# Splitting expert weights once and reloading the split pairs from HBM scratch

## The chip, the cores and the metric

The kernel runs on one core of one Trainium2 chip. The metric is device time in microseconds, the median of several runs. Engines are named as the profile names them: PE is TensorE (PEld its weight loads), DVE is VectorE, ACT is ScalarE, POOL is GpSimd, SP is SyncE, which here issues nearly all DMAs. A name with a q at its end (SPq) is the engine's sequencer: it waits and issues.

## The reference, cut to what matters

Attention with a compressive memory gives x; a mixture of four experts then runs on x.

```
B, H, S, D = 4, 8, 576, 64
a = softmax(causal(q @ k.T / sqrt(D)))
x = g * mem_out + (1 - g) * (a @ v)        # as (2304, 512)
N, D, E, F = 2304, 512, 4, 1024
p = domain_probs / (domain_probs.sum(-1) + 1e-9)
for e in range(E):
    h = np.maximum(x @ w1[e], 0.0)
    out += p[:, e:e+1] * (h @ w2[e])       # every token, every expert
```

All data are float32. The products keep that precision by splitting an operand into a high part (rounded to the fp32r format of TensorE) and a low part (the rest); a product is then three matmuls: high by high, high by low, low by high.

## The kernel before, in words

The tokens are cut into 9 groups of 256 (two tiles of 128 rows). Each group goes through 8 phases, one for each expert and half of F (`NPH` = 8). Group g starts at phase `START[g]` (0, 5, 8, 13, 16, 21, 24, 29, 32), so there are 40 phases (`PHASES`). In phases 0 to 4 and 37 to 39 one group is active (products of 256 columns), in phases 5 to 36 two groups are (512 columns).

One phase uses four pieces of w1 and four of w2, each 128x512 floats (256 KB). `mm1` makes h for each of the four pieces `fc` of w1: 4 x 3 matmuls each, then ACT (L769) and DVE (L770) split relu(h) into `hh` and `hl`. `mm2` makes y for each token tile: 4 x 3 matmuls with the w2 pieces, then DVE adds p*y to `acc` (L806); after a group's last phase `acc` is stored (L813).

A weight piece gets to its operand in this way. `w_dma` loads it on SP's queue into one of four staging tiles `stg` (L189 for w1, in runs of 512 bytes; L194 for w2, in runs of 2 KB). `w_prep` makes the high part (ACT L210, or POOL L212) and the low part (POOL L214; DVE for some pieces of the last four phases), then calls `w_dma` for the piece that comes four later, whose staging tile has just been read. `w_prep(i, "2")` is called after each piece of `mm1` of phase i, `w_prep(i + 1, "1")` after the tiles of `mm2` of phase i. The operands (`w1h`, `w1l`, `w2h`, `w2l`, four of each) exist once. `wseq` lists the pieces of all 40 phases in order, 320 in all: each expert's weights are loaded and split again every eight phases.

Batch 0's first 256 rows are computed in `first_run`, which also prepares the first eight pieces (on POOL). All other attention work is a list of steps of 28 tasks, interleaved with the phases by a planner with costs written by hand; a group's steps are all emitted before its first phase. A task's q, k and v come in by `t_load` (L269 and L275, tile `natall`, six or more DMAs on SP's queue), are transposed on PE (`tq`, `tk`, line L315), split, and partly copied by DMA from SBUF to SBUF (`kha`, `khb`, L342; `qz`, L361). The engines run in program order, and each DMA issue of SP waits in SP's own order until its source is ready and its destination free. The attention steps run through phase 28; later phases hold expert work alone.

Of the kernel before, what the change touches and what calls it, by code (L numbers as in the profile page):

```python
# [8 lines left out]
F32 = mybir.dt.float32  # L9
F32R = mybir.dt.float32r  # L10
# [12 lines left out]
PR = {  # L23
    "phi1": [-5, 1],
    "phi2": [-5, 7],
    "phi3": [-4, 7],
    "trq": [-3, 6.5],
    "trk": [-4, -0.5],
    "v": -2,
    "trqp": [2, 2.5],  # L30
    "qk": 0,
# [22 lines left out]
def tile_attention_moe(  # L54
# [13 lines left out]
    nc = tc.nc  # L68
    P = 128
    B, H, S, D = q.shape  # L70
    NT, DM = out.shape
    E, _, F = w1.shape
    NPAIR = H // 2
    NKD = DM // P
    HF = 4
# [20 lines left out]
    NPH = E * NHALF  # L96
    START = [g // 2 * NPH + (PR["x"] if g % 2 else 0) for g in range(NG)]
    PHASES = START[-1] + NPH
# [10 lines left out]
    def ctile(shape, dt, name):  # L109
        return cst.tile(shape, dt, tag=name, name=name)  # L110

    def f(ap):
        return ap.bitcast(F32)
# [4 lines left out]
    def wid(c):  # L118
        return min((c + 1) * P, S)
# [12 lines left out]
    for i in range(2):  # L132
        o, d = i * 13 * P, {}
# [25 lines left out]
    xl = ctile([P, NKD, 2 * GW], F32R, "xl")  # L159
    hh = [ctile([P, 2 * GW], F32R, f"hh{i}") for i in range(HF)]  # L160
    hl = [ctile([P, 2 * GW], F32R, f"hl{i}") for i in range(HF)]
    w1s = [
        (ctile([P, NKD, P], F32R, f"w1h{i}"), ctile([P, NKD, P], F32R, f"w1l{i}"))
        for i in range(HF)
    ]
    w2s = [
        (ctile([P, DM], F32R, f"w2h{i}"), ctile([P, DM], F32R, f"w2l{i}"))
        for i in range(HF)
    ]


    halves = [(i // NHALF % E, i % NHALF) for i in range(PHASES)]
    wseq = [(i, kind, fc) for i in range(PHASES) for kind in "12" for fc in range(HF)]
    NSTG = 4
    wpos = {"dma": 0, "prep": 0}
    stg = {}
# [1 line left out]
    def w_dma():  # L178
        j = wpos["dma"]
        if j >= len(wseq):  # L180
            return
        wpos["dma"] += 1
        i, kind, fc = wseq[j]
        e, hf = halves[i]
        f0 = (hf * HF + fc) * P
        t = sp.tile([P, DM], F32, tag="stg", name=f"stg{j}", bufs=NSTG)
        stg[j] = t
        if kind == "1":
            nc.sync.dma_start(  # L189
                out=t.rearrange("p (c f) -> p c f", c=NKD),  # L190
                in_=w1[e, :, f0 : f0 + P].rearrange("(c p) f -> p c f", p=P),
            )
        else:
            nc.sync.dma_start(out=t, in_=w2[e, f0 : f0 + P, :])  # L194

    def w_prep(i, kind, pool=False):
        last_ = i >= PHASES - 4
        act = (kind == "1" or i < START[1] or last_) and not pool
        j = wpos["prep"]
        if j >= len(wseq) or wseq[j][0] != i or wseq[j][1] != kind:  # L200
            return
        wpos["prep"] += 1
        fc = wseq[j][2]
        t = stg.pop(j)
        hi, lo = (w1s if kind == "1" else w2s)[fc]
        if kind == "1":
            hi = hi.rearrange("p c f -> p (c f)")
            lo = lo.rearrange("p c f -> p (c f)")
        if act:
            nc.scalar.activation(hi, t, AF.Copy)  # L210
        else:
            nc.gpsimd.tensor_scalar(hi, t, 1.0, 1.0, ALU.mult, ALU.mult)  # L212
        dve = (last_ and fc % 2) or (i < START[1] and fc < PR["lod"])
        (nc.vector if dve else nc.gpsimd).tensor_tensor(lo, t, f(hi), ALU.subtract)  # L214
        w_dma()


# [29 lines left out]
    for b, cs in RUNS[1:]:  # L247
        for a in range(NPAIR):
            t = Task()
# [146 lines left out]
    for t in tasks:  # L396
# [7 lines left out]
        for hds, c in order:  # L404
            s = Slot()
# [257 lines left out]
    def mm(n):  # L663
        return max(107.0, n / 2.4 + 2.5)
# [23 lines left out]
    for i, s in slots.items():  # L688
        w = wid(s.c)
        t = s.t  # L690
# [61 lines left out]
    def mm1(i, fc, cols, after):  # L752
        wh, wl = w1s[fc]
        pt = []

        def part(c):
            if c == 0:
                pt.append(ps.tile([P, 512], F32, tag="moe", name=f"h{i}_{fc}", bufs=3))
            for z, (w_, x_) in enumerate(((wh, xh), (wh, xl), (wl, xh))):
                nc.tensor.matmul(  # L760
                    pt[0][:, cols],
                    lhsT=w_[:, c],
                    rhs=x_[:, c, cols],
                    start=(c == 0 and z == 0),
                    stop=(c == NKD - 1 and z == 2),
                )
            if c == NKD - 1:
                h_, l_ = hh[fc][:, cols], hl[fc][:, cols]
                nc.scalar.activation(h_, pt[0][:, cols], AF.Relu)  # L769
                nc.vector.scalar_tensor_tensor(  # L770
                    l_, pt[0][:, cols], 0.0, f(h_), ALU.max, ALU.subtract
                )
                after()

        return [lambda c=c: part(c) for c in range(NKD)]

    def mm2(i, g, tt, after):
        e = halves[i][0]
        pieces = GROUPS[g][tt]
        pe = pn[:, pcol(pieces), e : e + 1]  # L780
        t0 = (g % 2) * GW + tt * P
        tk = slice(t0, t0 + P)
        pt = []

        def part(fc):
            if fc == 0:
                pt.append(ps.tile([P, 512], F32, tag="moe", name=f"y{i}_{g}_{tt}", bufs=3))
            wh, wl = w2s[fc]
            for z, (h_, w_) in enumerate(((hh, wh), (hh, wl), (hl, wh))):
                nc.tensor.matmul(  # L790
                    pt[0],
                    lhsT=h_[fc][:, tk],
                    rhs=w_,
                    start=(fc == 0 and z == 0),
                    stop=(fc == HF - 1 and z == 2),
                )
            if fc == HF - 1:
                fin()
                after()

        def fin():
            if i == START[g]:
                acc[g, tt] = sp.tile([P, DM], F32, tag="acc", name=f"acc{g}_{tt}", bufs=4)
                nc.vector.tensor_scalar(acc[g, tt], pt[0], pe, None, ALU.mult)
            else:
                nc.vector.scalar_tensor_tensor(  # L806
                    acc[g, tt], pt[0], pe, acc[g, tt], ALU.mult, ALU.add
                )
            if i == START[g] + NPH - 1:
                o0 = 0  # L810
                for b, c in pieces:
                    r0, m = b * S + c * P, rows(c)
                    nc.sync.dma_start(out=out[r0 : r0 + m, :], in_=acc[g, tt][o0 : o0 + m])  # L813
                    o0 += m

        return [lambda c=c: part(c) for c in range(HF)]

    def phase_parts(i):
        gs = [g for g in range(NG) if START[g] <= i < START[g] + NPH]
        c0 = min(g % 2 for g in gs) * GW  # L820
        cols = slice(c0, c0 + len(gs) * GW)
        out_ = []
        for fc in range(HF):
            for p_ in mm1(i, fc, cols, lambda: w_prep(i, "2")):
                out_.append((3 * mm(len(gs) * GW), p_))
        if i + 1 in START:
            out_.append((0.0, START.index(i + 1)))
        nt = 2 * len(gs)

        def after():  # L830
            for _ in range(HF // nt):
                w_prep(i + 1, "1")

        for g in gs:
            for tt in range(2):
                for p_ in mm2(i, g, tt, after):
                    out_.append((3 * mm(DM), p_))
        return out_


    def first_run():
# [226 lines left out]
        out=mask[:, 4 * P :],  # L1068
        in_=mask[:, 4 * P :],
# [24 lines left out]
    with tc.manual_schedule():  # L1094
# [8 lines left out]
        for i in range(2):  # L1103
            zeros(i)
            nc.gpsimd.memset(f(QK[i]["qz"]), 0.0)
            nc.gpsimd.memset(f(QK[i]["qa"][:, 3 * P :]), 0.0)
        phases = [phase_parts(i) for i in range(PHASES)]
        pcost = [sum(c for c, _ in ph) for ph in phases]

# [65 lines left out]
```

## Time and profile before

| what | value |
|---|---|
| median of 3 runs | 1035.13 us (1034.83 to 1036.03) |
| span of the profiled execution | 1034.4 us |
| PE busy | 1007.5 us, 97% |
| DVE, ACT, POOL busy | 688.3, 482.8, 582.6 us |
| DMA moved | 123.16 MB, mean 119 GB/s |
| mean share of time in which the 16 DMA engines worked, queue q1 (SP and ACT) | 43.3% |
| HBM read, written | 106.86 MB, 4.72 MB |

The profile gives the span from the first instruction to the last of one execution; the execution's own total is not recorded beside it, and the median of the runs is 0.7 us above the span. A busy PE is an engine with a matmul in its pipeline, so one matmul's duration (about 390 ns for 512 columns) is longer than the distance to the next.

### The profile page before, as it was taken

To read this page: it belongs to the slowest core of one execution; us is meant where nothing else is said; L and a number is where in the kernel's file an instruction comes from. 1 tells how busy PE (TensorE), PEld (TensorE's weight loads), DVE (VectorE), ACT (ScalarE), POOL (GpSimd) and SP (SyncE) were. 2 spreads that over 40 slices of the span, in tenths; PEclk is the share of its full clock that TensorE was granted. 3 is DMA by queue.
4 is the path that set the end of the run, shared out by engine and by line. 5 is a ranking of instruction groups with operands and counts; after the bars stand their busy time and mean duration, and the time that the engine had idled before them with its cause. 6 is when DMAs were issued, how large, how long until landed. Compare 5 with 4: busy or idle time off the path is not lost.

```text
span 1034.4 us, 16262 instructions
## 1 busy us (share of the span) xinstructions
PE 1007.5 (97%) x5183; PEld 846.1 (82%) x5183; DVE 688.3 (67%) x1638; ACT 482.8 (47%) x1144; POOL 582.6 (56%) x599
## 2 busy tenths in 40 slices
PE   6798999999999999999999999999999999999998
PEld 4588888888888888888888888888888888888887
DVE  6689887888777777887777867766666323222344
ACT  4476755565554555545555555444434222211234
POOL 4658566666544755467444565565553654656233
PEclk8899899999999999999999999999999999999999
DMA  6546554465434444355334544263331432333244
GB/s 139 128 129 188 154 156 114 122 165 131 114 96 120 132 130 109 88 145 140 101 94 103 139 128 119 79 174 87 92 103 57 128 102 82 123 101 94 79 142 134
DMA packets 213637, 123.16 MB, mean 119 GB/s; under 512 B 100656, under 2 KB 187696, under 8 KB 213552
## 3 DMA queue, kind: packets, MB, share of 16 engines
q1 hardware_dynamic: 213264, 121.85, 43.3%
q8 instruction: 42, 0.69, 0.3%
q10 hardware_dynamic: 288, 0.27, 0.1%
q14 instruction: 43, 0.35, 0.1%
HBM read 106.86 MB, written 4.72 MB: 108 GB/s over the span
## 4 chain that ended last, share of the span: by engine, by line
PE 87%; DVE 6%; POOL 3%; issue 2%; ACT 1%; DMA 1%; SPq 0%; POOLq 0%; ACTq 0%; DVEq 0%
PE y L790 36%; PE h L760 35%; PE sp L553 4%; PE pt L315 4%; PE o L654 4%; POOL w1l L214 1%; PE tk L315 1%; PE o L501 1%; PE tq L315 1%; DVE sf L943 1%; PE tp L315 1%; POOL w2l L214 1%; PE sp L427 1%; DVE qp L310 1%; DVE rn L308 0%
## 5 line engine op out<-in xcount | busy, mean ns | idle before, releaser
L214 POOL TENSOR_TENSOR w1l<-stg,w1h 128x512 fp32r<-128x512 f32 x152 | 198.2, 1315 | 314.3 <-ACT w1h L210 258.5
L760 PE MATMUL h<-xh,w1h 128*128 128x512 f32 (+1 forms) x640 | 248.5, 388 | 0.0
L760 PE MATMUL h<-xh,w1l 128*128 128x512 f32 (+1 forms) x640 | 237.8, 372 | 0.0
L790 PE MATMUL y<-w2h,hh 128*128 128x512 f32 x576 | 237.2, 412 | 0.0
L760 PE MATMUL h<-xl,w1h 128*128 128x512 f32 (+1 forms) x640 | 236.8, 370 | 0.0
L790 PE MATMUL y<-w2h,hl 128*128 128x512 f32 x576 | 226.8, 394 | 0.0
L790 PE MATMUL y<-w2l,hh 128*128 128x512 f32 x576 | 226.0, 392 | 0.7 <-POOL w2l L214 0.7
L214 POOL TENSOR_TENSOR w2l<-stg,w2h 128x512 fp32r<-128x512 f32 x152 | 198.8, 1311 | 46.4 <-ACT w2h L210 35.7
L769 ACT ACTIVATE hh<-h 128x512 fp32r<-128x512 f32 (+1 forms) x160 | 88.7, 555 | 237.9 <-PE h L760 236.5
L770 DVE SCALAR_TENSOR_TENSOR hl<-h,hh 128x512 fp32r<-128x512 f32 (+1 forms) x160 | 101.8, 636 | 125.4 <-ACT hh L769 124.2
L806 DVE SCALAR_TENSOR_TENSOR acc<-y,pn,acc 128x512 f32<-128x512 f32 x126 | 94.2, 748 | 73.5 <-PE y L790 72.7
L760 PEld LDWEIGHTS h<-xh,w1l 128*128 128x128 f32 x640 | 121.3, 190 | 21.4
L760 PEld LDWEIGHTS h<-xh,w1h 128*128 128x128 f32 x640 | 121.6, 190 | 16.5 <-issue 0.2
L760 PEld LDWEIGHTS h<-xl,w1h 128*128 128x128 f32 x640 | 121.9, 191 | 15.8
L790 PEld LDWEIGHTS y<-w2h,hl 128*128 128x128 f32 x576 | 108.7, 189 | 25.1 <-DVE hl L770 1.0
L790 PEld LDWEIGHTS y<-w2l,hh 128*128 128x128 f32 x576 | 109.5, 190 | 18.6 <-POOL w2l L214 1.1
L790 PEld LDWEIGHTS y<-w2h,hh 128*128 128x128 f32 x576 | 109.3, 190 | 18.0
L596 ACT ACTIVATE pth<-pt 128x384 fp32r<-128x384 f32 (+3 forms) x128 | 50.4, 420 | 103.4 <-PE pt L315 102.9
L210 ACT ACTIVATE w1h<-stg 128x512 fp32r<-128x512 f32 x156 | 93.6, 624 | 9.2 <-DMA stg<-in_moe_w_dram 8.4
L212 POOL TENSOR_SCALAR w2h<-stg 128x512 fp32r<-128x512 f32 x128 | 81.8, 639 | 15.9 <-PE y L790 15.9
L561 DVE CUSTOM_DVE_ANT_0 s<-sp,mask 128x384 f32<-128x384 f32 (+1 forms) x96 | 52.9, 563 | 13.4 <-PE sp L553 12.7
L315 PE MATMUL pt<-ident,s 128*128 128x128 f32 (+1 forms) x376 | 60.9, 273 | 0.4 <-DVE s L464 0.4
(152 smaller groups left out, 1425.1 us busy)
## 6 DMA issues: line engine op xcount, KB each, us to landing
stg<-in_moe_w_dram SPq DMA_DIRECT2D x320, 256.0 KB, 2.9
natall<-in_k_dram SPq DMA_DIRECT2D x34, 128.0 KB, 2.7
out_dram<-acc SPq DMA_DIRECT2D x16, 256.0 KB, 2.2
natall<-in_v_dram SPq DMA_DIRECT2D x32, 128.0 KB, 2.6
natall<-in_q_dram SPq DMA_DIRECT2D x60, 64.0 KB, 2.7
kha<-kha SPq DMA_DIRECT2D x16, 128.0 KB, 3.2
khb<-khb SPq DMA_DIRECT2D x16, 128.0 KB, 3.0
natall<-in_k_dram SPq DMA_DIRECT2D x28, 64.0 KB, 2.4
```

Of the source, the lines that this page charges most:

```text
L210: nc.scalar.activation(hi, t, AF.Copy)
L212: nc.gpsimd.tensor_scalar(hi, t, 1.0, 1.0, ALU.mult, ALU.mult)
L214: (nc.vector if dve else nc.gpsimd).tensor_tensor(lo, t, f(hi), ALU.subtract)
L315: nc.tensor.transpose(dst, src, ident[0:n, 0:n])
L553: nc.tensor.matmul(pt[:, 0 : b_ - a], lhsT=q_, rhs=qk[k_][:, a:b_], start=y == 0, stop=y == len(pairs) - 1,)
L561: nc.vector.tensor_tensor_reduce(s.s[:, a:b_], pt[:, 0 : b_ - a], mask[:, m0 : m0 + b_ - a] if c < 4 else mask4[:, a:b_], 1.0, 3.0e38, ALU ...
L596: nc.scalar.activation(dh, src, AF.Copy)
L760: nc.tensor.matmul(pt[0][:, cols], lhsT=w_[:, c], rhs=x_[:, c, cols], start=(c == 0 and z == 0), stop=(c == NKD - 1 and z == 2),)
L769: nc.scalar.activation(h_, pt[0][:, cols], AF.Relu)
L770: nc.vector.scalar_tensor_tensor(l_, pt[0][:, cols], 0.0, f(h_), ALU.max, ALU.subtract)
L790: nc.tensor.matmul(pt[0], lhsT=h_[fc][:, tk], rhs=w_, start=(fc == 0 and z == 0), stop=(fc == HF - 1 and z == 2),)
L806: nc.vector.scalar_tensor_tensor(acc[g, tt], pt[0], pe, acc[g, tt], ALU.mult, ALU.add)
```

## The change

Only the 64 pieces of phases 0 to 7 are loaded and split (`wseq` ends at `NPH`). High and low part of a piece now lie side by side in one tile `wpair` of 128x2x512 floats. After each split the pair is noted in `wpend`; the next call of `w_prep` first stores what is noted to a DRAM tile of its own (`w_store`, 512 KB on SP's queue). From phase 8 on `w_load` brings a pair from its DRAM tile straight into the operands, again on SP's queue, 512 KB each: a w1 pair of phase i+1 right after `mm1` of phase i has used that piece, the four w2 pairs together after the last tile of `mm2` of phase i. The rule for the last four phases (`last_`: ACT and DVE help) is gone.

```diff
+    wpair = {k_: [ctile([P, 2, DM], F32R, f"w{k_}{i}") for i in range(HF)] for k_ in "12"}
...
-    wseq = [(i, kind, fc) for i in range(PHASES) for kind in "12" for fc in range(HF)]
+    wseq = [(i, kind, fc) for i in range(NPH) for kind in "12" for fc in range(HF)]
+    wkeep = {}
+    wpend = []
...
+    def w_store():
+        while wpend:
+            key, t = wpend.pop(0)
+            d = tc.dram_tile([P, 2, DM], F32, name="wk%d%s%d" % key)
+            wkeep[key] = d
+            nc.sync.dma_start(out=d, in_=f(t))
+
+    def w_load(i, kind, fc):
+        if NPH <= i < PHASES:
+            nc.sync.dma_start(out=f(wpair[kind][fc]), in_=wkeep[i % NPH, kind, fc])
+
     def w_prep(i, kind, pool=False):
-        last_ = i >= PHASES - 4
-        act = (kind == "1" or i < START[1] or last_) and not pool
+        w_store()
+        act = (kind == "1" or i < START[1]) and not pool
...
-        dve = (last_ and fc % 2) or (i < START[1] and fc < PR["lod"])
+        dve = i < START[1] and fc < PR["lod"]
...
+        wpend.append((wseq[j], wpair[kind][fc]))
         w_dma()
...
-            for p_ in mm1(i, fc, cols, lambda: w_prep(i, "2")):
+            def after1(fc=fc):
+                w_prep(i, "2")
+                w_load(i + 1, "1", fc)
+
+            for p_ in mm1(i, fc, cols, after1):
...
+        left = [nt]
+
         def after():
             for _ in range(HF // nt):
                 w_prep(i + 1, "1")
+            left[0] -= 1
+            if left[0] == 0:
+                for fc in range(HF):
+                    w_load(i + 1, "2", fc)
```

`PR["lod"]` is 0, so `dve` is false in the changed kernel.

## Rows read from the trace of the kernel before

**Rows 1.** The page, engines: busy us, share of the span, instructions.
```profile
PE 1007.5 (97%) x5183; PEld 846.1 (82%) x5183; DVE 688.3 (67%) x1638; ACT 482.8 (47%) x1144; POOL 582.6 (56%) x599
```
**Rows 2.** Windows: length, then busy us of each engine, granted clock, DMA.
```profile
core 0: us, PE busy (x) PEld busy (x) DVE busy (x) ACT busy (x) POOL busy (x), PEclk, DMA share, GB/s
...
60.40:130.20 69.80, 63.37 (x411) 57.05 (x410) 62.70 (x154) 51.16 (x135) 51.77 (x52) 0.95 0.62 170
130.20:215.20 85.00, 84.67 (x449) 70.88 (x448) 71.94 (x192) 48.49 (x131) 53.53 (x63) 1.00 0.49 135
215.20:803.60 588.40, 587.36 (x3018) 493.92 (x3017) 440.55 (x1056) 294.06 (x680) 330.34 (x328) 1.00 0.43 114
803.60:996.90 193.30, 193.30 (x854) 159.94 (x854) 56.50 (x82) 44.47 (x80) 101.12 (x95) 1.00 0.36 105
996.90:1030.50 33.60, 33.60 (x216) 30.41 (x214) 16.93 (x29) 15.90 (x32) 13.03 (x10) 1.00 0.47 142
```
**Rows 3.** The chain of work that ended last, 803 us on: start, us, what.
```profile
811.88 10.88 PE y L790 x48
...
996.87 5.75 PE h L760 x48
```
**Rows 4.** Timeline of PE: the first matmul of phases 1, 5 and 8.
```profile
60.40 0.28 PE L760 MATMUL h<-xh,w1h 128*128 128x256 f32 x1
...
130.21 0.47 PE L760 MATMUL h<-xh,w1h 128*128 128x512 f32 x1
...
215.23 0.40 PE L760 MATMUL h<-xh,w1h 128*128 128x512 f32 x1
```
**Rows 5.** Waits of PE: us in total, times, longest.
```profile
PE y L790 <- POOL w2l L214: 0.7, 1, 0.7
```
**Rows 6.** The page, costliest groups: the split's instructions on ACT and POOL.
```profile
L214 POOL TENSOR_TENSOR w1l<-stg,w1h 128x512 fp32r<-128x512 f32 x152 | 198.2, 1315 | 314.3 <-ACT w1h L210 258.5
...
L210 ACT ACTIVATE w1h<-stg 128x512 fp32r<-128x512 f32 x156 | 93.6, 624 | 9.2 <-DMA stg<-in_moe_w_dram 8.4
L212 POOL TENSOR_SCALAR w2h<-stg 128x512 fp32r<-128x512 f32 x128 | 81.8, 639 | 15.9 <-PE y L790 15.9
```
**Rows 7.** The page, DMA issues: count, KB each, median us to landing.
```profile
stg<-in_moe_w_dram SPq DMA_DIRECT2D x320, 256.0 KB, 2.9
```
**Rows 8.** DMA between 60.4 and 130.2 us (phases 1 to 4).
```profile
DMA packets 20598, 11.87 MB, mean 170 GB/s; under 512 B 9169, under 2 KB 18385, under 8 KB 20591
...
stg<-in_moe_w_dram SPq DMA_DIRECT2D x33, 256.0 KB, 3.0
```
**Rows 9.** DMA between 130 and 215 us (phases 5 to 7).
```profile
DMA packets 19765, 11.47 MB, mean 135 GB/s; under 512 B 10055, under 2 KB 17479, under 8 KB 19757
...
stg<-in_moe_w_dram SPq DMA_DIRECT2D x25, 256.0 KB, 2.9
```
**Rows 10.** Windows: one lone 256 KB store of `acc`; the fastest microsecond.
```profile
1029.40:1030.30 0.90, 0.90 (x5) 0.58 (x4) 0.00 (x0) 0.00 (x0) 0.00 (x0) 1.00 0.76 291
...
1022.00:1023.00 1.00, 1.00 (x11) 1.00 (x10) 0.37 (x1) 0.51 (x2) 1.00 (x1) 1.00 1.05 395
```
**Rows 11.** DMA issues between 30 and 36 us.
```profile
stg<-in_moe_w_dram SPq DMA_DIRECT2D x4, 256.0 KB, 5.9
```
**Rows 12.** Timeline of SP: a task's k loads being issued.
```profile
73.80 0.97 SPq L269 DMA_DIRECT2D natall<-in_k_dram  x2
```
**Rows 13.** Timeline of PE: the transposes that read those k loads.
```profile
77.81 0.41 PE L315 MATMUL tk<-ident,natall 128*128 128x128 f32 x2
```
**Rows 14.** Windows: the four microseconds behind a wait of PE.
```profile
104.00:108.00 4.00, 4.00 (x20) 3.54 (x20) 2.73 (x9) 2.70 (x6) 1.76 (x2) 0.79 0.64 166
```
**Rows 15.** Timeline of DVE: one small instruction of two tasks.
```profile
47.22 0.16 DVE L308 SCALAR_TENSOR_TENSOR rn<-rn,gate 128x4 f32<-128x4 f32 x1
...
66.82 0.95 DVE L308 SCALAR_TENSOR_TENSOR rn<-rn,gate 128x4 f32<-128x4 f32 x1
```
**Rows 16.** Waits of SP's queue: us in total, times, longest.
```profile
SPq L194 <- POOL w1l L214: 251.8, 109, 12.1
```

More of the change, by code (lines that the diff above doesn't have):

```diff
@@ L161, in tile_attention_moe @@
     hl = [ctile([P, 2 * GW], F32R, f"hl{i}") for i in range(HF)]
+    wpair = {k_: [ctile([P, 2, DM], F32R, f"w{k_}{i}") for i in range(HF)] for k_ in "12"}
     w1s = [
-        (ctile([P, NKD, P], F32R, f"w1h{i}"), ctile([P, NKD, P], F32R, f"w1l{i}"))
-        for i in range(HF)
-    ]
[L166 to L169, printed above, removed]
+        tuple(t[:, z].rearrange("p (c f) -> p c f", c=NKD) for z in range(2)) for t in wpair["1"]
+    ]
+    w2s = [tuple(t[:, z] for z in range(2)) for t in wpair["2"]]
     halves = [(i // NHALF % E, i % NHALF) for i in range(PHASES)]
-    wseq = [(i, kind, fc) for i in range(PHASES) for kind in "12" for fc in range(HF)]
+    wseq = [(i, kind, fc) for i in range(NPH) for kind in "12" for fc in range(HF)]
+    wkeep = {}
+    wpend = []
     NSTG = 4
```

## The prediction

> **What bounds the kernel now.** I read the page's engine rows first: PE is busy 97% of the span, no other engine above 67% [rows 1]. The windows say where PE is not full. In phases 1 to 4 it idles 69.80 - 63.37 = 6.4 us; in phases 5 to 7 0.3 us; from phase 8 to the end of the attention work 588.40 - 587.36 = 1.0 us; after 803 us nothing [rows 2, 4]. The chain of waits agrees: late it is PE alone, 48 matmuls in 10.88 us, 0.227 us each, and 5.75 us for the 48 narrow ones of a half phase [rows 3]. While PE runs at that pace, POOL is still splitting weights (101.12 us of 193.30 [rows 2]). So the splits cost PE nothing there. In the list of waits, PE waits for a split once, 0.7 us [rows 5]. Two other things matter for this change: the DMA engines work 0.62 of the time in phases 1 to 4, 0.49 in phases 5 to 7 and 0.36 to 0.47 later [rows 2], and SP's queue is mostly held back by POOL's splits [rows 16].
>
> **What is removed.** The 256 pieces of phases 8 to 39 lose an ACT or POOL copy (0.62 to 0.64 us) and a subtraction of 1.3 us [rows 6]. That is over 300 us of POOL work, none of it on PE's path. The most that can come back is PE's idle time from phase 8 on, 1.0 us [rows 2]. I take -1.0. Lower bound of the cost: -3, if the wait of 0.7 us [rows 5] and its like also cost refills of the pipeline that count as busy; upper bound: 0.
>
> **What is added in phases 0 to 7: 64 stores of 512 KB.** SP issues them in front of the next staging load. No row shows a 4 KB row or a 512 KB transfer, so I bound the price. A lone 256 KB store moves at 291 GB/s in 0.9 us, which makes 1.80 us for 512 KB; the fastest microsecond of the trace moved 395 GB/s, which makes 524,288 / 395e3 = 1.33 us [rows 10]. I take 1.33, because these stores run in a filled queue, like that microsecond and unlike the lone one.
>
> Phases 1 to 4 (69.8 us) issue 33 staging loads and so 33 stores, beside the 11.87 MB that they move already [rows 8]. Stores: 33 x 1.33 = 43.9 us. The old transfers need at least 11.87e3 / 395 = 30.1 us and at most 0.62 x 69.8 = 43.3 us. The share counts overlapping packets twice (it is 1.05 in the fastest microsecond [rows 10]), so I take the lone store's pace, 11.87e3 / 291 = 40.8 us. Sum: 84.7 us of DMA work in 69.8 us, 14.9 too many. The bounds: 30.1 + 43.9 = 74.0, 4 too many; 43.3 + 33 x 1.80 = 102.7, 33 too many.
>
> Phases 5 to 7 have room: 11.47e3 / 291 + 25 x 1.33 = 72.7 of 85 us [rows 9, 2]. How much backlog can be carried there? The staging ring holds four pieces; four loads of 0.9 and four stores of 1.33 would be 8.9 us in the queue. I take half, 5 us. That leaves +10 us in phases 1 to 4.
>
> Why does PE feel it, though stores are needed by nobody for a long time? All transfers sit in SP's one queue. Four staging loads that are issued at the end of a burst of transfers near 30 us land after 5.9 us instead of 2.9 [rows 11, 7]; a load behind two or three stores will fare the same. What is late next is named in the rows: a task's k loads finish being issued at 74.77 us, and PE's transposes of them start at 77.81, 3.0 us later, hardly more than a landing [rows 12, 13, 7]. These transposes stand in PE's program order, so expert matmuls behind them wait too. The staging loads come late as well; then ACT's copy waits, and behind it, in ACT's order, the evictions of h and the exponentials. SP itself pays 0.97 / 2 = 0.49 us for an issue [rows 12], 16 us for 33 stores. It already waits in the same places for POOL's subtraction [rows 16], so the store brings no new wait for data.
>
> After a wait PE's clock drops: behind one of the present waits the granted clock is 0.79 of 2.4 GHz over 4 us, a loss of 0.21 x 4 = 0.8 us [rows 14]. New waits in four phases would cost 3 us. Against that, the 6.4 us that PE already idles there [rows 2] can fall together with the new waits. I count the two as equal: 0, bounds -4 and +4. Before phase 1 eight stores fall into the start, where the weights are ready long before they are used; 0, upper bound 2.
>
> The Trainium skill, "DMA: Bandwidth & Descriptors", section "Where 436 GB/s comes from", says that transfers between HBM and SBUF are held by HBM at about 358 GB/s for a core. By that figure a store would be 1.46 us, an estimate, and the sum 40.8 + 33 x 1.46 = 89.0 us, so +14 after the carried 5 in place of +10. The fastest microsecond here, 395 GB/s [rows 10], is above it.
>
> **What is added from phase 8 on: 256 loads of 512 KB** instead of 256 KB. Per full phase that is 8 x 1.33 = 10.6 us (bound 8 x 1.80 = 14.4) for 8 x 0.9 = 7.2 us before, in 21.8 us of pure expert work [rows 3, 10]. The shares of 0.43 and 0.36 [rows 2] rise by 0.15 to 0.33: not full. A w1 pair has most of a phase to arrive. The four w2 pairs are issued together when y ends: 4 x 1.33 to 4 x 1.80 plus the fixed 2.9 - 0.9 = 2.0 us gives 7.3 to 9.2 us for the last. In full phases 10.88 us of h cover that. In the three half phases the cover is 5.75 us, plus nine matmuls of y before the fourth pair is used, 2.0 us: 7.8 us [rows 3]. So 0 to 1.4 us each; I take 0, upper bound 4. SP now waits for PE at each load instead of for POOL; behind it stand the loads of later tasks and the copies `kha`, `qz`, whose sources come from PE work emitted later, so I take 0. Upper bound 5, if some q, k or v loads fall behind a burst of w2.
>
> **Sum.** -1 + 10 + 0 + 0 = +9 us on the span of 1034.4. The median of the runs is 0.7 us above the span, so 1035.1 + 9 = **1044 us**.
>
> **Rivals.**
> *The stores hide (no change).* For it: nobody needs them soon, and by the lowest bound only 4 us are too many, which the staging ring can carry into phases 5 to 7. Against it: the k loads with no slack [rows 12, 13]. Time: 1035.1 - 1 + 0 to 2 = 1034 to 1036.
>
> *Faster: DVE and POOL stop colliding.* One small DVE instruction takes 0.16 us in one task and 0.95 in another [rows 15]. If a POOL instruction holds it up, then without the splits every DVE step of the attention chain from phase 8 on is shorter. This decides only if PE waits for that chain; PE's idle 1.0 us says it does not [rows 2]. With the -3 above and hidden stores: 1032. The Trainium skill, "SBUF — State Buffer", section "Who interferes with whom", says that a DVE instruction with two SBUF inputs contends with a GpSimd instruction that reads SBUF. The 0.16 and 0.95 us agree with such a lock, but a freed DVE is not what PE lacks here.
>
> *Much slower: the loads hurt too.* Stores at 1.80 us (+33 - 5 = +28), or bursts of w2 that hold up task loads and the half phases (+9 above the sum). Time 1053 to 1063. For it: the small packets in phases 1 to 4 (9,169 of 20,598 under 512 bytes [rows 8]). Against it: later shares stay under 0.8.
>
> *The change doesn't do what it says:* the DRAM pairs are stored long before phase 8 and the loads name them directly; I see no way and give it nothing.
>
> **How the numbers follow.** Forecast (the early phases are held by DMA, +2 to +17, 1037 to 1052): 0.60. Stores hidden: 0.14. Faster: 0.10. Much slower: 0.16. A change under 0.2% (2.1 us) can't be told from none here. Slower by more: 0.60 + 0.16 = 0.76; the same 0.14; faster 0.10. For 8 in 10 I leave out the faster case and the upper half of the much slower one: 1034 to 1058; the forecast's own range is 1037 to 1052.
>
> **What would show it.** In the changed profile: DMA share near 0.9 or above from about 60 to 200 us; staging loads there landing after 4 to 7 us instead of 3.0; phase 8 starting near 225 us instead of 215.2; PE waiting at `tk` or ACT at L287 and L210 for landings. From phase 8 on, POOL under 150 us busy, stretches of PE as long as before (588 and 193 us), DMA share 0.55 to 0.7. Wrong would be: phase 8 starting at 215 us (the stores hide), or the half phases longer than 33.6 us, or PE waiting for `w2` loads after phase 8.

## The result, and the profile after

The change makes the kernel slower: 1048.88 us (median of 4 runs) against 1035.58 us (median of 4 runs of the kernel before), a ratio of 1.0128 [1.0114 to 1.0143], or +13.3 us. The forecast was 1044.0 us, with a range of 1034 to 1058 and 0.76 on slower. The profiled execution of the changed kernel took 1048.86 us for a span of 1047.1 us. Against the span before, 1034.4 us, that is +12.7 us. The distance of 0.7 us between span and median in the prediction was not that of one execution, where it is 1.8 us here.

These are rows of the changed kernel's page: the engines, the DMA share in 40 slices of 26.2 us, a group of the split, and the two new transfers (count, KB each, median us to landing).

```profile
PE 1010.6 (97%) x5183; PEld 848.9 (81%) x5183; DVE 640.4 (61%) x1622; ACT 406.5 (39%) x1000; POOL 201.1 (19%) x247
...
DMA  6879998896657656567546666575644565545666
...
L224 POOL TENSOR_TENSOR w<-stg,w 128x512 fp32r<-128x512 f32 x64 | 83.7, 1312 | 46.6 <-ACT w L220 36.4
...
w<-wk SPq DMA_DIRECT2D x256, 512.0 KB, 4.7
wk<-w SPq DMA_DIRECT2D x64, 512.0 KB, 5.0
```

The edit does what it says. There are 64 subtractions by POOL, 64 stores and 256 loads, and POOL falls from 582.6 [rows 1] to 201.1 us. PE's busy share doesn't move. The DMA row has its nines early, between some 80 and 240 us, and never again.

To place the time I cut the span where the first matmul of a phase starts, as in [rows 4]. These are windows of the changed kernel: phases 1 to 4, 5 to 7, 8 to the end of the attention work, the pure expert work, the three half phases, and then the first two stretches of phase 5.

```profile
core 0: us, PE busy (x) PEld busy (x) DVE busy (x) ACT busy (x) POOL busy (x), PEclk, DMA share, GB/s
...
61.40:142.20 80.80, 67.28 (x412) 60.22 (x410) 58.64 (x155) 51.76 (x134) 52.09 (x52) 0.92 1.00 341
142.20:229.65 87.45, 85.61 (x449) 70.80 (x447) 70.81 (x194) 48.39 (x131) 50.11 (x60) 1.00 0.92 296
229.65:815.60 585.95, 585.95 (x3016) 494.02 (x3015) 408.05 (x1053) 249.55 (x597) 66.06 (x82) 1.00 0.60 188
815.60:1009.10 193.50, 193.50 (x858) 160.25 (x856) 53.84 (x77) 23.44 (x40) 0.00 (x0) 1.00 0.57 195
1009.10:1043.20 34.10, 33.98 (x217) 30.40 (x215) 9.60 (x18) 4.60 (x12) 0.00 (x0) 1.00 0.81 308
...
142.20:152.00 9.80, 8.49 (x48) 6.90 (x46) 7.14 (x19) 4.80 (x13) 8.80 (x10) 1.00 1.03 384
152.00:162.00 10.00, 9.77 (x50) 7.81 (x48) 7.82 (x23) 6.28 (x16) 4.08 (x6) 1.00 0.94 284
```

Read against [rows 2, 4], this gives a ledger. Phase 1 starts at 61.40 instead of 60.40 us: +1.0. Phases 1 to 4 take 80.80 instead of 69.80 us: +11.0. Phases 5 to 7 take 87.45 instead of 85.0 us: +2.4. From phase 8 to the end of the attention work it is 585.95 instead of 588.40 us, -2.4; the pure expert work +0.2 and the three half phases +0.5. The sum is +12.7 us, all of the span's difference. The loss lies where the stores are; from phase 8 on, where the 256 larger loads are, 0.7 us are lost and 2.4 won.

In phases 1 to 4 the DMA engines are full (share 1.00, before 0.62). PE idles 13.5 us there instead of 6.4, and what it does takes 3.9 us longer at a mean granted clock of 0.92 instead of 0.95. This is the DMA view of that stretch (packets; then count, KB each, median us to landing):

```profile
DMA packets 24220, 27.59 MB, mean 341 GB/s; under 512 B 9404, under 2 KB 18108, under 8 KB 24213
...
wk<-w SPq DMA_DIRECT2D x32, 512.0 KB, 5.0
stg<-in_moe_w_dram SPq DMA_DIRECT2D x33, 256.0 KB, 5.1
...
natall<-in_k_dram SPq DMA_DIRECT2D x8, 64.0 KB, 3.2
```

The same 33 staging loads as in [rows 8] land after 5.1 us instead of 3.0. The waits of PE in the same stretch (us in total, times, longest) name what PE feels:

```profile
PE tk L326 <- DMA natall<-in_k_dram: 6.5, 2, 5.2
PE o L512 <- DVE ptl L498: 3.0, 3, 1.4
PE tk L326 <- DVE s L475: 2.6, 1, 2.6
```

The first wait is new; it is the transposes of the k tiles that [rows 13] showed. The third is put down to DVE, but it is the same place: by the trace's records the last k load lands at 81.49 us and PE starts right behind it, at 81.62, as in the first. So PE waits 9.1 us of its 13.5 for k loads. They land only a little later after their issue, 3.2 us in place of 2.5. They are late because they are *issued* late: those that phase 3 needs were issued 3.6 us before that phase began in the kernel before (89.67 and 93.28 us), and 1.8 us after it began here (99.75 and 97.92). SP's timeline of the changed kernel shows what holds SP up (start, duration):

```profile
101.80 0.47 SPq L200 DMA_DIRECT2D wk<-w  x1
102.61 0.34 SPq L193 DMA_DIRECT2D stg<-in_moe_w_dram  x1
102.99 0.63 SPq L200 DMA_DIRECT2D wk<-w  x1
103.72 0.42 SPq L193 DMA_DIRECT2D stg<-in_moe_w_dram  x1
104.18 1.16 SPq L200 DMA_DIRECT2D wk<-w  x1
```

The first store there, right behind a task's small loads, occupies SP for 0.47 us, the third for 1.16 us. Summed over phases 1 to 4, 107 issues take 70.8 of SP's 80.8 us; in the kernel before 76 issues took 34.8 of 69.8 us. The chain that ends just after 145 us runs through the same place:

```profile
105.45 0.44 SPq L193
105.89 0.04 issue
105.93 6.77 DMA wk<-w
112.72 1.15 SPq L200
113.87 0.05 issue
113.96 5.89 DMA stg<-in_moe_w_dram
119.87 0.37 SPq L280
```

Here a store that was issued at 105.93 us lands after 6.77 us, and only then does SP issue the store at 112.72; a staging load's flight ends, and only then does SP issue a task's load (L280). SP is not still in between: it issues seven other DMAs during the first flight. In the trace's records the DMAs of SP's queue tell of their landing by eight semaphores in turn, and none of them starts before the eighth before it has landed (849 cases in the changed kernel). This rule seldom binds here: in phases 1 to 4 SP stands still for a landing in five places, 1.8 us in all. What makes it late is that it issues nearly without a pause.

### The profile page after: what moved, and what is told of

The parts are those of the page before. It is cut to its first block, busy times and chain, and to the rows that moved or that the text cites. A ratio compares the mean times of both kernels' runs of the same rounds, so it can differ in the third digit from the quotient of the medians.

```text
span 1047.1 us, 15578 instructions
## 1 busy us (share of the span) xinstructions
PE 1010.6 (97%) x5183; PEld 848.9 (81%) x5183; DVE 640.4 (61%) x1622; ACT 406.5 (39%) x1000; POOL 201.1 (19%) x247
## 4 chain that ended last, share of the span: by engine, by line
PE 84%; DMA 5%; POOL 3%; issue 3%; SPq 2%; DVE 2%; ACT 1%; POOLq 0%; ACTq 0%; DVEq 0%
PE y L801 35%; PE h L771 34%; PE sp L564 4%; PE pt L326 3%; PE o L665 3%; DMA stg<-in_moe_w_dram 3%; POOL w L224 2%; DMA wk<-w 1%; SPq L200 1%; PE tk L326 1%; PE tq L326 1%; PE tp L326 1%; DMA zb<-in_z_prev_dram 1%; PE sp L438 0%; PE o L512 0%
## 5 line engine op out<-in xcount | busy, mean ns | idle before, releaser
L771 PE MATMUL h<-xh,w 128*128 128x512 f32 (+1 forms) x1280 | 412.1, 382 | 1.2 <-DVE hl L781 1.2
L801 PE MATMUL y<-w,hh 128*128 128x512 f32 x1152 | 369.2, 401 | 0.2
L771 PEld LDWEIGHTS h<-xh,w 128*128 128x128 f32 x1280 | 237.9, 192 | 39.3 <-DVE hl L781 1.4
L771 PE MATMUL h<-xl,w 128*128 128x512 f32 (+1 forms) x640 | 237.9, 372 | 0.0
L801 PEld LDWEIGHTS y<-w,hh 128*128 128x128 f32 x1152 | 206.7, 189 | 36.3 <-POOL w L224 0.8
L801 PE MATMUL y<-w,hl 128*128 128x512 f32 x576 | 226.4, 393 | 0.1
L817 DVE SCALAR_TENSOR_TENSOR acc<-y,pn,acc 128x512 f32<-128x512 f32 x126 | 94.3, 748 | 81.5 <-PE y L801 80.5
L771 PEld LDWEIGHTS h<-xl,w 128*128 128x128 f32 x640 | 123.0, 192 | 15.7
L801 PEld LDWEIGHTS y<-w,hl 128*128 128x128 f32 x576 | 108.4, 188 | 24.8 <-DVE hl L781 0.6
L224 POOL TENSOR_TENSOR w<-stg,w 128x512 fp32r<-128x512 f32 x64 | 83.7, 1312 | 46.6 <-ACT w L220 36.4
L588 ACT ACTIVATE s<-s,st 128x384 f32<-128x384 f32 (+2 forms) x80 | 54.8, 685 | 0.5 <-DVE st L583 0.2
```

The costliest lines, as they stand in the source:

```text
L588: nc.scalar.activation(s.s[:, 0:w], s.s[:, 0:w], AF.Exp, bias=s.st[:, 0:1], scale=-1.0, accum_out=s.st[:, 2:3],)
L771: nc.tensor.matmul(pt[0][:, cols], lhsT=w_[:, c], rhs=x_[:, c, cols], start=(c == 0 and z == 0), stop=(c == NKD - 1 and z == 2),)
L801: nc.tensor.matmul(pt[0], lhsT=h_[fc][:, tk], rhs=w_, start=(fc == 0 and z == 0), stop=(fc == HF - 1 and z == 2),)
L817: nc.vector.scalar_tensor_tensor(acc[g, tt], pt[0], pe, acc[g, tt], ALU.mult, ALU.add)
```

## The experiments

My theory: the stores' bytes fill the DMA engines in phases 0 to 7, and PE pays through k and staging loads that arrive late. The rivals: the 64 more issues on SP cost the time, not the bytes; the place of the stores in SP's queue does; or the larger loads from phase 8 on do. All edits are to the changed kernel. The kernel before ran on the same chips, with medians of 1034.72 to 1034.84 us.

### The stores taken away, made small, halved

```diff
-            d = tc.dram_tile([P, 2, DM], F32, name="wk%d%s%d" % key)
-            wkeep[key] = d
-            nc.sync.dma_start(out=d, in_=f(t))
+            if key[0] == 0:
+                d = tc.dram_tile([P, 2, DM], F32, name="wk%d%s%d" % key)
+                wkeep[key] = d
+                nc.sync.dma_start(out=d, in_=f(t))
+            else:
+                d = tc.dram_tile([P, 2, 8], F32, name="wk%d%s%d" % key)
+                nc.sync.dma_start(out=d, in_=f(t)[:, :, 0:8])
...
-            nc.sync.dma_start(out=f(wpair[kind][fc]), in_=wkeep[i % NPH, kind, fc])
+            nc.sync.dma_start(out=f(wpair[kind][fc]), in_=wkeep[0, kind, fc])
```

This is the run with tiny stores. The run without stores has no `else`; the one with half stores writes the high part alone there, `in_=f(t[:, 0])`, to a tile of 128x512.

No store after phase 0. 

> Only the eight pairs of phase 0 are stored; all later loads read these eight, so the weights from phase 8 on are not the reference's; count, size and time of the loads are those of the change. Theory (the 56 stores of phases 1 to 7 fill the DMA engines): phases 1 to 7 as long as before, phase 8 starts at 215 to 218 us in place of 229.7, DMA share in phases 1 to 4 near 0.6, and from phase 8 on the 817 us of the changed kernel: median 1034 to 1037. Rival (what costs is something else in the early phases, such as the new tiles or the changed order of SP's queue): phase 8 still near 230 us and 1047 to 1049. Rival (the loads cost too): later part longer than 819 us.

56 stores of 8 KB. 

> As the run without stores, but phases 1 to 7 issue their 56 stores with 8 columns of each half in place of 512 (8 KB in place of 512 KB); later loads read phase 0's eight pairs. Theory (bytes on the DMA engines): 1034 to 1038. Rival (SP's time for 56 more issues of about 0.4 us and their places among the transfers that may be under way): most of the 14 us stay, 1044 to 1049.

56 stores of 256 KB. 

> As above, but the 56 stores of phases 1 to 7 write the high half alone, 256 KB. Theory (a queue that is overfull): phases 1 to 4 move 11.9 + 33 x 0.26 = 20.5 MB, at the 341 GB/s of the changed kernel 60 us of 69.8, so the engines are not full any more: 1035 to 1040, less than half of the loss. A price that is proportional to the bytes gives 1042; a price for each store 1047 to 1049.

And, the other way, each pair stored twice (a second `dma_start` to a DRAM tile of its own). 

> The change, with each pair stored twice, to two DRAM tiles: 128 stores. Theory (the engines are full, so more bytes cost their whole time): phases 1 to 4 move 27.6 + 33 x 0.52 = 44.9 MB, at 341 GB/s 132 us in place of 81, phases 5 to 7 25.9 + 24 x 0.52 = 38.5 MB, 113 us at 341 GB/s in place of 87; total 1110 to 1130. A price that is proportional to the stores, with no full engine: 1049 + 13 = 1062.

Measured: without stores 1033.49 us (ratio 0.9984 [0.9971 to 0.9997]); tiny 1036.59 us, half 1035.01 us, double 1124.41 us (one execution each; the ten without stores spread over 5.1 us, so two or three us between single executions say little). The theory's ranges hold, but for the run without stores, 0.5 us below its own. Windows of phases 1 to 4, in this order:

```profile
62.87:128.87 66.00, 60.37 (x412) 54.40 (x410) 60.09 (x152) 49.84 (x133) 50.33 (x51) 1.00 0.62 176
```
```profile
61.88:130.88 69.00, 61.83 (x412) 54.59 (x410) 60.23 (x152) 50.51 (x133) 50.48 (x51) 1.00 0.70 171
```
```profile
59.00:128.92 69.92, 61.58 (x412) 54.51 (x410) 60.53 (x152) 50.84 (x133) 50.36 (x51) 1.00 0.92 282
```
```profile
69.44:189.28 119.84, 77.68 (x412) 66.87 (x410) 54.75 (x155) 52.20 (x133) 51.44 (x52) 0.81 1.01 361
```

Multiply length by share to get the DMA engines' work: 40.9 us without stores, 48.3 tiny, 64.3 half, 80.8 as changed, 121 double. Now compare with the length. As long as the work is below some 66 to 70 us, the stretch ends near 130 us whatever the DMA engines do. Above that the length *is* the work: 80.8 and 119.84 us. (With a share of 1.00 that holds by definition, so the price of a store is the better test.) Half stores add 23.4 us of work in a stretch with room, 0.73 us each; from none to all, 32 stores add 39.9 us, 1.25 us each; from all to double, 30 more stores (the window has 62) add 40.2 us, 1.34 us each. The price is nearly linear, the time lost is not: no stores, tiny and half ones cost the stretch nothing against the 69.8 us of before [rows 2], all of them 11, double ones 50 us. (The double run's total was right by luck: the stretch was forecast at 132 us and took 119.84, phases 5 to 7 took 116.2 instead of 113, and phase 1 began 8 us later than as changed.)

Two rivals fall. 56 tiny stores leave every issue on SP and bring phase 8 to 217.75 us instead of the 215.47 us without stores, so the issues by themselves are worth some 2 us of the 14, no more than single executions differ. The loads from phase 8 on are all there in the run without stores, and it is not slower than the kernel before. In the run with double stores PE's list of waits is led by the place that the changed kernel showed:

```profile
PE tk L328 <- DMA natall<-in_k_dram: 51.0, 7, 15.2
```

### The stores moved out of SP's queue

```diff
-            nc.sync.dma_start(out=d, in_=f(t))
+            nc.scalar.dma_start(out=d, in_=f(t))
```

> The change, with the 64 stores issued from ACT's DMA queue in place of SP's; bytes and counts are the same. Theory A (the engines have too much to move, whatever the order): DMA share in phases 1 to 4 stays near 1.0 and the time at 1045 to 1050. Theory B (the loads suffer because they stand behind the stores in one queue, the stores themselves are not urgent): the loads pass the stores, staging loads land after about 4 us, phases 1 to 4 take 70 to 75 us, 1035 to 1042. ACT pays for 64 issues of about 0.4 us in its own order.

Measured: 1069.98 us (one execution), outside both ranges. Phases 1 to 4 take 90.7 us and 5 to 7 take 93.6; phase 1 starts at 66.7 us. From the DMA view of phases 1 to 4 (packets, MB, share of 16 engines), and ACT's longest wait between 40 and 160 us:

```profile
q1 hardware_dynamic: 20410, 11.57, 47.5%
q10 hardware_dynamic: 4519, 16.41, 45.4%
...
wk<-w ACTq DMA_DIRECT2D x32, 512.0 KB, 4.5
```
```profile
ACT w L220 <- POOL w L224: 22.5, 14, 2.9
```

The two queues keep the engines busy 0.93 of the time in sum, 84 us of work, so the bytes cost what they did. The Trainium skill, "DMA: Bandwidth & Descriptors", section "Issuing engines are not separate DMA queues", says just that: transfers from several issuing engines run on the same 16 DMA engines, and only issue time is saved. The two shares, 47.5% and 45.4%, are consistent with that, as they stay below 1 together; they do not prove it. SP's own issues take 42.0 us there instead of 70.8, and the stretch is longer all the same. What is new is ACT's waiting: a store needs POOL's subtraction, and in ACT's order everything behind the store waits with it. That this alone explains the 21 us over the changed kernel was not separated.

### The stores put right behind a task's loads

```diff
-    def w_store():
-        while wpend:
+    def w_store(most=6):
+        while len(wpend) > most:
...
         if NPH <= i < PHASES:
+            w_store(0)
```

A further `w_store(0)` stands at the end of `t_load`, behind a task's loads.

> The change with the same 64 stores in another order: up to six finished pairs are held back and stored right after a task's q, k and v loads have been issued, so that these loads stand in front of the stores. Theory A (bytes alone): phases 1 to 4 must move 27.6 MB, 74 us at the 375 GB/s of the run that stores twice, 81 at the 341 of the change, so at best 4 us of the 11 come back there: 1040 to 1049. Theory B (place in SP's queue): the k loads come as early as before, 1035 to 1039. Worse than the change (above 1049), if six stores in a row hold up the staging loads behind them.

Measured: 1073.37 us, ratio 1.0378 [1.0363 to 1.0392]: far worse than leaving them where they were. A window of phases 1 to 4, and SP's timeline:

```profile
59.26:152.41 93.15, 74.09 (x411) 64.15 (x410) 60.38 (x152) 48.90 (x130) 49.84 (x51) 0.85 0.84 272
```
```profile
100.32 7.00 SPq L200 DMA_DIRECT2D wk<-w  x7
107.41 4.45 SPq L193 DMA_DIRECT2D stg<-in_moe_w_dram  x4
```

The DMA engines are *less* full, 0.84, and yet the stretch is 12 us longer than as changed. The new order did what theory B asked of it: PE does not wait for k loads in this stretch at all. The loss came by a way that none of my theories had. These are ACT's longest wait in the stretch, two of PE's, and ACT's wait of the same kind in phases 1 to 4 of the changed kernel:

```profile
ACT w L221 <- DMA wk<-w: 18.7, 8, 4.2
```
```profile
PE o L514 <- DVE ptl L500: 6.3, 4, 2.7
PE h L773 <- POOL w L225: 4.2, 6, 0.9
```
```profile
ACT w L220 <- DMA wk<-w: 1.4, 1, 1.4
```

L221 writes a new high part into the operand that the store of the old pair reads, so it waits until that store has landed. A store that is held back lands late; then ACT and POOL split late, and PE waits for splits and for steps of the attention on DVE and ACT. SP's burst is there too: seven stores in a row hold SP for 7.0 us, and four staging loads behind them another 4.45. But SP stands still for a landing only 0.9 us in this stretch, against 21.8 us in which its staging loads wait for POOL. So a store has a second price beside the engines' time: the operand that it reads is not free until it has landed. (The 375 GB/s of the expectation is 361 in the window.)

### The stores given to passes in which the DMA engines are less busy

The weights are split twice (phases 0 to 15), stored in the second pass and loaded from phase 16 on:

```diff
-    wseq = [(i, kind, fc) for i in range(NPH) for kind in "12" for fc in range(HF)]
+    wseq = [(i, kind, fc) for i in range(2 * NPH) for kind in "12" for fc in range(HF)]
...
-        if NPH <= i < PHASES:
+        if 2 * NPH <= i < PHASES:
...
+        if i >= NPH:
             wpend.append((wseq[j], wpair[kind][fc]))
```

> The weights are split in phases 0 to 15, the stores are made in phases 8 to 15 alone, and pairs are loaded from phase 16 on. Theory (a store costs only where the DMA engines have no room): phases 8 to 15 work at a share of 0.43 + 0.36 = 0.8, so the stores hide; phases 0 to 7 are as before; the gain of 1 to 2 us in phases 8 and 9, where PE no longer waits for splits, is lost as well: 1034 to 1036, no change. Rival (a store costs 13 / 64 = 0.2 us wherever it stands): 1047 to 1049.

The same with three passes, the stores in phases 16 to 23 (`3 * NPH`, `2 * NPH`). 

> As the run with the stores in the second pass, but one pass later: pieces are split in phases 0 to 23, stored in phases 16 to 23, loaded from phase 24 on. In the kernel before, the k loads of the tasks in phases 16 to 23 are there 5 to 9 us before PE's transposes, in phases 8 and 9 only 0.3 to 2 us. Theory (a store costs what it adds to the lateness of a task's loads beyond this slack): phases 8 to 23 as long as before, 1034 to 1036. Rival (the second pass lost its 2 us to the stores themselves): again about 1036.5 to 1037.

And half of each: the w2 pairs stored in phases 0 to 7 and loaded from 8; w1 split again, stored in 8 to 15 and loaded from 16. 

> Half of the stores in each pass: w2 pairs are stored in phases 0 to 7 and loaded from phase 8 on, w1 pieces are split again in phases 8 to 15, stored there and loaded from phase 16 on. Theory: phases 1 to 4 move 11.9 + 16 x 0.52 = 20.3 MB, as with half stores, which cost nothing there; phases 8 and 9 keep the gain of w2 pairs that are ready: 1033 to 1035. Rival (bursts of 512 KB stores hold up the loads, though the sum fits): 1038 to 1043.

Measured: second pass 1036.62 us, ratio 1.0021 [1.0012 to 1.0030], 0.6 us above its range; third pass 1034.95 us, ratio 1.0002 [0.9993 to 1.0011]; half of each 1054.58 us, ratio 1.0184 [1.0167 to 1.0201], where I had expected no loss, and above the rival's range too.

In the profiled execution of the second pass, the slowest of its eleven (1038.98 us), all phases but one last as before; phase 9 takes 31.8 instead of 29.5 us. PE's wait for the loads between 244 and 264 us shows most of it:

```profile
PE tk L327 <- DMA natall<-in_k_dram: 1.9, 1, 1.9
```

It is the same place again, once in eight phases. With the third pass no such wait for a task's loads is left, and nothing is gained either.

The miss teaches most. With half the stores in phases 0 to 7 the start of phase 8 moves by 3.8 us only, to 218.98. But phase 8 takes 37.7 instead of 29.6 us, and phases 12 and 13 lose 2.5 and 4. A window of phase 8, the chain there, and PE's wait:

```profile
218.98:256.70 37.72, 30.72 (x154) 25.62 (x153) 23.76 (x63) 17.41 (x45) 12.69 (x18) 0.91 0.67 208
```
```profile
225.17 0.43 SPq L209
225.61 0.05 issue
225.70 8.51 DMA w<-wk
234.22 3.08 DMA natall<-in_k_dram
237.30 0.14 issue
237.43 1.09 PE tk L332 x4
```
```profile
PE tk L332 <- DMA natall<-in_k_dram: 7.0, 1, 7.0
```

The DMA share is 0.67. The engines have room; SP has none. The four w2 loads that are issued together come between stores of w1, one of them flies 8.51 us, and only when it has landed is the k load issued, the eighth DMA behind it, which takes 3.08 us more. Here the rule of eight binds: SP stands still four times for a w2 load, 4.5 us in all.

## Why the prediction was right, and which terms were off

*The mechanism* was as forecast. The transfers of phases 1 to 4 are more than fits, and the k loads bring it to PE: share 1.00 until 142 us and 0.92 until 230 (forecast: near 0.9 from 60 to 200), staging loads at 5.1 us (4 to 7), PE waiting at `tk`.

*Phases 1 to 4* were given +10 and cost +11.0. The price of a store was 1.33 us and measured 1.25 in engine work; the old transfers were taken as 40.8 us and measured 40.9 without stores. The demand of 84.7 us was 80.8. The 5 us that were to be carried into phase 5 were not carried on balance: the length equals the demand. Two errors of 4 to 5 us cancel there, so that +10 came so near is luck. By the Trainium skill's figure of 358 GB/s ("DMA: Bandwidth & Descriptors", section "Where 436 GB/s comes from") the term would have been +14, an estimate. The sustained 341 GB/s here, and 361 with double stores, lie near that figure, while a store's 1.25 us is nearer to the 1.33 from the fastest microsecond than to its 1.46.

*Phases 5 to 7* are the term that failed: 0 against +2.4 us, and with it the sum. There was room in all, as said (work 0.92 x 87.45 = 80.5 us, below the 85.0 of before). The loss is in phase 5 alone, 30.9 us instead of 28.6; phases 6 and 7 are as before. Phase 5 begins with a share of 1.03, and PE idles 1.3 of its first 9.8 us, so a backlog carried into it suggests itself. The runs do not bear that out. Without stores phase 5 takes 30.2 us, with tiny stores 30.5, with half stores 30.2, though without stores the share of its first ten us is about 0.5. PE's wait is the same, as changed and without stores:

```profile
PE o L512 <- DVE ptl L498: 1.3, 1, 1.3
```
```profile
PE o L513 <- DVE ptl L499: 1.3, 1, 1.3
```

In the runs with the second and third pass, where nothing is stored in phases 0 to 7, phase 5 takes 28.6 us. In the three runs without, with tiny and with half stores, phase 4 is 0.5 to 2.6 us shorter than before, so PE may just come too early for DVE there; in the changed kernel it is 2.5 us longer. So whether the backlog or DVE's step costs the 2.3 us stays open.

*The start* was 0 with a bound of 2 and cost +1.0 us. That is not resolved: phase 1 starts between 59.0 and 62.9 us in most of the other runs, with and without stores. In phase 0 PE waits 4.5 us for k loads, but it did so in the kernel before: the profile has 3.9 us there and names DVE, and the last k load lands 0.14 us before PE starts in both.

*Clock against idle time* was counted as equal. In phases 1 to 4 PE's busy time grew by 3.9 us at the lower clock and its idle time by 7.1; together they are the 11.0 that the demand gave, so a term of its own was not needed.

*From phase 8 on* the forecast was -1.0 and it was -1.7: phases 8 and 9 are 0.9 and 0.8 us shorter, in all runs that load pairs there but the one with half of each. In the kernel before, PE's idle time, 1.0 us, was not the most that could come back: 2.4 us came back by the end of the attention work, 1.4 of it out of time counted as busy. The three half phases are 0.5 us longer together, within the bound of 1.4 each. Two signs of being wrong show, both slightly: those phases take more than 33.6 us, and in the last one PE waits 0.2 us for the fourth w2 pair, which lands 7.7 us after its issue. Hidden splits were worth next to nothing to PE although POOL lost 380 us of work. The run without stores bounds it: with all that the change could give, and only the loads and the first eight stores of its price, the kernel is 0.16% faster.

*How PE comes to wait* was half right. I had the loads land late behind stores; the k loads are mostly issued late, because SP is still issuing. That step hung on the fixed issue time of 0.49 us [rows 12], 16 us for 33 stores; the 32 stores took SP 26.4 us, and all its issues 36 us more than before. It did not change the sum here, where the engines are full as well. SP's standing still for landings, which I did not have at all, decided the run with half of each, where I missed. Nor did I have the operand that a store holds: nobody waits for the stored pair, but the next split waits for its operand, 1.4 us in the changed kernel and 18.7 us where stores were held back.

What stays open: how the loss in phases 1 to 4 splits between full engines and SP's longer issues, since every edit that moved one moved the other; what makes phase 5 longer; and how much of the loss with ACT's queue is ACT's waiting.

## What to carry to other kernels

Add up the DMA work of a stretch (length times share, plus the new transfers at the pace of the fastest microsecond) and compare it with the stretch's length: below it the stores cost next to nothing here, unless something waited behind them, above it every microsecond of work was paid. An engine's work that never stands on PE's path, here 380 us of POOL, buys nothing when it goes, so ask first what pays for its removal. A burst of large transfers on one queue delays the small loads behind it even where the engines have room, so look at what is issued next, not only at the average share. A store also holds the buffer that it reads until it has landed: ask who writes that buffer next.

## What was not expected of the hardware

An issue on SP's queue is not of fixed length. A 512 KB store takes 0.47 us to issue right behind a task's small loads and 1.16 us two stores later, with fewer than eight transfers under way. Apart from that, each issue comes only after the landing of the eighth DMA before it (6.77 and 8.51 us after that one's start in the chains above), without an exception in all runs whose stores go out on SP's queue. Whether the chip or the way in which the program was built sets the eight was not tried.

Stores of 8 KB in rows of 32 bytes cost the DMA engines about (48.3 - 40.9) / 32 = 0.23 us each, for a sixty-fourth of the bytes whose store costs 1.25 us.
